# An S4 + MLP block on one core: packed parameters by way of DRAM in whole tiles, stores of u on two queues, and every DMA of the planned stage placed by the plan

## The chip, the core and the metric

The kernel runs on one NeuronCore of a Trainium2 chip. The metric is the device time of one execution in microseconds (us). Five engines work from instruction streams of their own, each in order: TensorE (PE, with its weight loads as PEld), VectorE (DVE), ScalarE (ACT), GpSimd (POOL) and SyncE (SP). SP and POOL here issue transfers for the most part; those are carried out by 16 DMA engines.

## The reference

One adaLN block over x of 2048 positions by 512 channels: a state-space convolution (S4) and an MLP with Mish, each behind a layer norm that is scaled, shifted and gated by a condition.

```python
mod = (silu(c) @ w_mod).reshape(1, 6, 1, -1)
sa, ca, ga, sb, cb, gb = (mod[:, i] for i in range(6))
h = layernorm(x) * (1 + ca) + sa
x = x + ga * A(h)
h = layernorm(x) * (1 + cb) + sb
return x + gb * (mish(h @ w1 + b1) @ w2)

def A(u):                                   # 512 channels d, 128 states n
    dt = exp(log_dt)
    P = exp(dt * (A_re + 1j*A_im) * arange(L))      # per d and n
    K = einsum("dn,dnl,dn->dl", C, P, dt * B).real  # the filter
    return causal_convolution(u, K) + u * Dskip     # by FFT over 2L
```

## The kernel before, in words

The 512 channels are four **blocks** of 128. For each block the kernel makes the filter's transform from the parameters, transforms u, multiplies the two, and transforms back; the results are added to x in DRAM (`x2d`). Then the MLP runs over four tiles of 512 positions. A first part of some 50 us (parameters of block 0, row statistics, the first modulation vectors) is written out by hand, and so is a `drain` (line 1154) that carries the last eight steps and leads over to the MLP. Between them lies the **planned stage**, which the change touches.

Its work is cut into operations of a few instructions, named by a short key and a number. Filter steps k = 0..31, eight to a block:

- `ang` k (TensorE, tile `pang`): angles of the powers, from the parameter tiles `S12` (in the trace all tiles `s...` go by the name `s`). `sin` k (ScalarE, into `ec`): three activations.
- `mag`, `comb` k (VectorE): `m` from `cf`, then four multiplications into `ec`. `cf` and `co` come from `vt` (TensorE, `pco`, from the tiles `S3`) and `va` (ScalarE, exponentials), four of each for a block.
- `kgen`, `ks`, `ka`, `tm` k (TensorE, ScalarE, TensorE, ScalarE): sums over states and the transform, kept in `gk`.

Convolution steps v = 0..31, eight to a block too, v being possible when filter steps 8b to 8b+7 of its block b are done:

- `gl` v (SP): load of `gu` from `ud`. `ubu`, `ug` v (TensorE `pub`, ScalarE): transform of u. `ubk` v (TensorE `pkb`): the last stage of the filter's transform.
- `prod` v (VectorE): two products and a sum, from `pkb` and `ug`. `t1`, `yt`, `invb`, `z` v: back-transform, and a store of `z` to `zd` in DRAM; `invb` uses the constants `mi` (`lm`, a load on POOL).
- per half block: `zl` (loads of `zt` from `zd`), `xp` (loads of x), `inva` (TensorE `pia`), `add` (VectorE) and the store to `x2d`.

Once, ahead of all `gl`: `ua` (TensorE `pua`) and `us` (ScalarE) make the first stage of u's transform in 32 pieces; each piece goes to `ud` in DRAM with two stores of 64 partitions, both on SP (line 773).

Parameters of blocks 1 to 3: `lp` loads the raw rows, `p0` to `p5` and `pa` (VectorE, with `p1` and the arctangent `pa` on ScalarE) compute them and write 12 rows for each of 128 partitions into the tile `pk`; `modp` rows (`mo`) are modulation vectors. `ls` spreads `pk` over the tiles `S3` and `S12`, whose partition is another one. For block 0 TensorE does that with selection matrices. For blocks 1 to 3 `ls` is 48 small copies from SBUF to SBUF on POOL: 32 for the first half of a block (lines 518 and 520, needed by its first `ang` and by `vt`) and 16 for the second.

**What sets the order.** `_plan` (line 57) is a list scheduler that runs on the host: each operation has an engine, a cost in `NS`, a place in `LEAD` or `AT` (smaller goes first), what it waits for with a lag, and the banks of PSUM that it takes. It hands back one sequence. The operations are then written out in that sequence, and for VectorE, ScalarE and TensorE a wrapper `InOrder` (line 286) holds the instructions to it. Transfers on SP and POOL were not held: they were issued inside the operation that makes their data (`z`, `us`, `add`), or stood in the plan at a cost near nothing (`gl`, `zl`, `lo`), and got their place in their queue from the framework's scheduler, by priority and its own estimates.

Of the kernel before, what the change touches and what calls it, by code (L numbers as in the profile page):

```python
# [39 lines left out]
NS = {"ang": 1400, "sin": 2900, "mag": 1140, "comb": 3570, "kgen": 1110, "ks": 270, "ka": 620, "tm": 560, "ubu": 1010,  # L40
      "ug": 770, "ubk": 1020, "prod": 1760, "t1": 590, "yt": 490, "invb": 1000, "z": 500, "inva": 1060, "add": 1210,
# [4 lines left out]
LEAD = {"ang": -1.72, "sin": -14.83, "mag": 4.37, "comb": 8.2, "kgen": 8.11, "ks": 1.94, "ka": -7.81, "tm":  # L46
        -0.64, "ubu": 15.3, "ug": 8.99, "ubk": 12.65, "prod": 4.12, "t1": 11.98, "yt": 10.08, "invb": 8.19, "z":
        11.51, "inva": 23.63, "add": 15.62}
AT = {"ua": -0.95, "un": 3.34, "nr": -2.74, "lf": 9.56, "na": 6.67, "sr": 0.11, "sg": 10.72, "st": -1.67,
# [3 lines left out]
SWITCH, HOP, LOAD, PART, TURN, STORE = 1280, 160, 4500, 2600, 5500, 3300  # L53
# [3 lines left out]
def _plan(k0):  # L57
    ops = {}

    def op(key, engine, pri, deps=(), banks=0, frees=None, table=None):  # L60
        ops[key] = (engine, NS[key[0]], pri, [d if len(d) == 3 else (*d, HOP) for d in deps], banks, frees, table)

# [36 lines left out]
    for v in range(nk - 6):  # L99
        op(("gl", v), "S", v + 5.6, [("ubu", v - 4) if v > 3 else ("mm", 0), ("us", 31, STORE)])  # L100
# [6 lines left out]
    for v in range(nk - 9):  # L107
# [11 lines left out]
    for b in range(1, nb):
        k = 8 * b  # L120
        if b:
# [160 lines left out]
def s4_block(ctx, tc, io, out):  # L282
    nc = tc.nc
    ordered = {key: None for key in "VAT"}
# [213 lines left out]

    def load_s(b, half):
        pk = PKR[b]  # L500
        for g in (half, 2 + half):
# [12 lines left out]
            for k in range(4):  # L514
                q = slice(32 * k, 32 * k + 32)
                if half == 0:
                    for i in (g, g + 1):
                        nc.gpsimd.dma_start(S3[b, i][q, :], pk[32 * i:32 * i + 32, 8 + k, :])  # L518
                for e in range(2):
                    nc.gpsimd.dma_start(S12[b, g][64 * e + 16 * k:64 * e + 16 * k + 16].rearrange("p h n -> p (h n)"),  # L520
                                        pk[d, k + 4 * e, :])
# [244 lines left out]
    def us(p):  # L766
# [5 lines left out]
        for h in range(2):  # L772
            US["last"] = nc.sync.dma_start(view(ud, (16 * a + 8 * h + g) * P, [[64 * P, 64], [64 * 64 * P, NB], [1, P]]),
                                           t[64 * h:64 * h + 64])

    def s_gl(v):
        b, s = divmod(v, 8)
        GU[v] = cv.tile([P, 512], F32, tag="gu", name=f"gu{v}", bufs=4).rearrange("p (r d) -> p r d", r=4)
        nc.sync.dma_start(GU[v], view(ud, (64 * b + 8 * s) * 64 * P, [[P, P], [P * P, 4], [1, P]]))
# [59 lines left out]
    def s_invb(v, whole=True):  # L839
# [703 lines left out]
```

## Time and profile before

| | us |
|---|---|
| median of 3 runs | 707.25 (706.45 to 708.76) |
| the profiled execution, its own time | 707.84 |
| its span, first to last instruction | 706.1 |
| first part, to the first row of the planned stage on VectorE | 0 to 49.7 |
| planned stage, to the last `add` | 49.7 to 343.9 |
| drain, to the first matmul of the MLP | 343.9 to 396.3 |
| MLP | 396.3 to 706.1 |

What the profiled execution takes beyond its span is 1.74 us. In the views, a row reads: start, length, engine, line, operation, output <- inputs with shapes, how many instructions; in brackets the idle time of that engine ahead of the row and what ended it. Nearly all rows have line 294, the wrapper's. A table of stretches gives, for each stretch, its length and the busy time of each engine with the number of instructions, then the granted clock of TensorE as a share, the share of the DMA engines and the rate. ScalarE and VectorE overlap the end of an instruction with the start of the next by some 0.1 us, so that lengths add up to a little more than the distance of starts.

### The profile page before, as it was taken

The page shows a single profiled execution, that of the slowest core. Times are in us where ns is not written, and L with a number is a line of the kernel's source. Part 1 is how long each engine was busy: PE and PEld are TensorE (multiplying, and loading weights), DVE is VectorE, ACT ScalarE, POOL GpSimd, SP SyncE. Part 2 cuts the span into 40 slices and gives each one's busy share as a digit, 9 for nine tenths or more (in the row PEclk, how much of TensorE's full clock was granted, in tenths as well). Part 3 has the DMA queues.
Part 4 walks back from the last instruction along what each step waited for, and adds up shares of the span by engine and source line. Part 5 has one row for each costly group of instructions (what it writes and reads, how often), then busy time and mean ns, then how long its engine had stood idle before and what let it go on. Part 6 is the DMA issues. An engine that isn't in the chain of part 4 may idle for free.

```text
span 706.1 us, 16609 instructions
## 1 busy us (share of the span) xinstructions
PE 616.7 (87%) x6722; PEld 497.4 (70%) x6722; DVE 478.5 (68%) x938; ACT 402.7 (57%) x705; POOL 102.0 (14%) x214
## 2 busy tenths in 40 slices
PE   0579796488888879899888999999999999999997
PEld 0445443367676657767786588889898888989996
DVE  7979961499869976979574899858237733563333
ACT  3677855488688856878572575453336234443231
POOL 2000058003900291000100000001001010010000
PEclk9968996699999997999999999999999999999999
DMA  9960579724435574764598799747433763264332
GB/s 251 219 256 15 138 200 213 234 78 127 113 107 139 146 178 128 195 173 121 157 277 260 230 320 298 244 142 225 129 102 93 205 176 94 90 180 144 96 90 59
DMA packets 108588, 117.31 MB, mean 166 GB/s; under 512 B 13408, under 2 KB 85472, under 8 KB 107360
## 3 DMA queue, kind: packets, MB, share of 16 engines
q1 hardware_dynamic: 93664, 85.61, 41.7%
q0 software_dynamic: 14464, 30.11, 15.2%
q8 instruction: 53, 0.87, 0.6%
q10 hardware_dynamic: 384, 0.52, 0.3%
q14 instruction: 23, 0.19, 0.1%
HBM read 81.36 MB, written 32.51 MB: 161 GB/s over the span
## 4 chain that ended last, share of the span: by engine, by line
PE 55%; DMA 13%; DVE 10%; issue 9%; ACT 7%; POOL 4%; SPq 1%; DVEq 0%; ACTq 0%; POOLq 0%
PE pr L294 31%; PE pp L294 11%; DVE ec L294 4%; DMA s<-pk 4%; ACT ec L294 3%; PE pang L294 3%; DMA zt<-zd 3%; DMA xr<-in_A_u 2%; POOL s L518 2%; PE pkg L294 2%; POOL s L520 2%; DVE q L294 2%; DMA zd<-z 2%; PE pib L294 1%; PE pia L294 1%
## 5 line engine op out<-in xcount | busy, mean ns | idle before, releaser
L294 PE MATMUL pr<-hh,w 128*128 128x256 f32 (+1 forms) x420 | 78.2, 327 | 0.5 <-ACT hh L294 0.5
L294 ACT ACTIVATE ec<-pang 128x1024 f32<-128x1024 f32 x64 | 62.3, 1027 | 27.0 <-PE pang L294 27.0
L294 PEld LDWEIGHTS pr<-hh,w 128*128 128x128 f32 x420 | 66.5, 188 | 12.7 <-ACT hh L294 1.9
L294 DVE TENSOR_TENSOR mh<-x,pr 128x256 f32<-128x256 f32 x63 | 26.4, 418 | 65.2 <-PE pr L294 64.9
L294 PE MATMUL pp<-w,mah 128*128 128x512 f32 x224 | 70.4, 396 | 0.0
L294 PE MATMUL pr<-w,mah 128*128 128x512 f32 x224 | 69.9, 393 | 0.0
L1265 POOL DMA_DIRECT2D w<-w2d x42 | 22.2, 528 | 301.7 <-PE pp L294 301.7
L294 DVE TENSOR_TENSOR ec<-ec,m 128x1024 f32<-128x1024 f32 x64 | 61.2, 957 | 3.5 <-ACT ec L294 1.0
L294 ACT ACTIVATE mh<-mh,b 128x256 f32<-128x256 f32 x63 | 32.1, 510 | 51.9 <-DVE mh L294 51.6
L294 ACT ACTIVATE mh<-pr,b 128x256 f32<-128x256 f32 (+1 forms) x35 | 19.4, 558 | 66.2 <-PE pr L294 66.2
L518 POOL DMA_DIRECT2D s<-pk x48 | 24.0, 503 | 181.4 <-PE pua L294 86.1
L294 DVE TENSOR_TENSOR m<-cf 128x1024 f32<-128x1024 f32 x32 | 38.9, 1217 | 16.4 <-ACT cf L294 16.4
L294 DVE TENSOR_TENSOR mal<-mh,mah 128x512 fp32r<-128x512 f32 x56 | 38.5, 688 | 14.6 <-ACT mah L294 14.5
L520 POOL DMA_DIRECT2D s<-pk x96 | 47.5, 501 | 4.9 <-DMA s<-pk 2.8
L294 PEld LDWEIGHTS pkg<-ec 128*32 128x32 f32 x2048 | 35.8, 117 | 16.5 <-issue 7.9
L294 PE MATMUL pkg<-ec 128*32 128x64 f32 x2048 | 41.0, 235 | 6.7 <-DVE ec L294 5.6
L294 PE MATMUL pub<-mf,gu 128*128 128x128 f32 x256 | 37.8, 294 | 10.4 <-issue 9.8
L294 ACT ACTIVATE ug<-pub,gd 128x512 f32<-128x512 f32 x64 | 34.0, 588 | 19.7 <-PE pub L294 19.5
L294 PE MATMUL pp<-w,mal 128*128 128x512 f32 x112 | 43.9, 392 | 0.0
L294 PE MATMUL pr<-w,mal 128*128 128x512 f32 x112 | 43.9, 392 | 0.0
L294 PEld LDWEIGHTS pub<-mf,gu 128*128 128x128 f32 x256 | 33.6, 204 | 13.0 <-issue 11.3
L294 PEld LDWEIGHTS pp<-w,mah 128*128 128x128 f32 x224 | 38.3, 189 | 4.9
(171 smaller groups left out, 1389.6 us busy)
## 6 DMA issues: line engine op xcount, KB each, us to landing
w<-w2d POOLq DMA_DIRECT2D x42, 512.0 KB, 3.6
ud<-us SPq DMA_DIRECT2D x64, 128.0 KB, 2.8
gu<-ud SPq DMA_DIRECT2D x32, 256.0 KB, 3.1
zd<-z SPq DMA_DIRECT2D x32, 256.0 KB, 2.7
zt<-zd SPq DMA_DIRECT2D x32, 256.0 KB, 5.2
w2d<-w SPq DMA_DIRECT2D x14, 512.0 KB, 4.1
xf<-x2d SPq DMA_DIRECT2D x16, 256.0 KB, 4.9
x2d<-xp SPq DMA_DIRECT2D x14, 256.0 KB, 3.6
```

The costliest lines, as they stand in the source:

```text
L294: ins = f(*a, **kw)
L518: nc.gpsimd.dma_start(S3[b, i][q, :], pk[32 * i:32 * i + 32, 8 + k, :])
L520: nc.gpsimd.dma_start(S12[b, g][64 * e + 16 * k:64 * e + 16 * k + 16].rearrange("p h n -> p (h n)"), pk[d, k + 4 * e, :])
L1265: nc.gpsimd.dma_start(t, w2d[f])
```

## The change

1. **`ls` by way of DRAM.** When `p5` has filled `pk`, a new operation `ps` stores the whole tile (128 partitions of 6 KB) to a DRAM buffer `pkd`, on SP. `ls` then loads whole tiles of 128 partitions from it on POOL: for the first half of a block four tiles `S3` and two tiles `S12`, for the second half two tiles `S12`. That is one store and eight loads for a block where there were 48 copies.
2. **Stores of u on two queues.** Of the two stores of a piece one is `ud` on SP, the other `up` on POOL.
3. **Every DMA is an operation.** `ud`, `up`, `zs` (store of z), `xs` (store to `x2d`) and `ps` are operations of their own, with costs; SP and POOL get an `InOrder` of their own, so that the plan's sequence is the queue's.
4. **Other numbers.** `NS`, `LEAD`, `AT` and the lags are new throughout, so that the sequence on every engine of the planned stage is another one. The arithmetic and the number of operations on VectorE, ScalarE and TensorE stay; ScalarE loads a table 12 times in both.

```diff
-LEAD = {"ang": -1.72, "sin": -14.83, "mag": 4.37, "comb": 8.2, ...
+LEAD = {"ang": 0.48, "sin": -8.01, "mag": 11.89, "comb": 2.1, ...
-SWITCH, HOP, LOAD, PART, TURN, STORE = 1280, 160, 4500, 2600, 5500, 3300
+SWITCH, HOP, LOAD, PART, TURN, STORE = 1280, 160, 4800, 3300, 5800, 3500
...
-            op(("us", p), "A", at + AT["us"], [("ua", g), ("us", p - 1), ("us", p - 8, STORE)], frees=[("ua", g)])
+            op(("us", p), "A", at + AT["us"], [("ua", g), ("us", p - 1), ("ud", p - 8, STORE), ("up", p - 8, STORE)],
+               frees=[("ua", g)])
+            op(("ud", p), "S", at + AT["us"], [("us", p)])
+            op(("up", p), "P", at + AT["us"], [("us", p)])
...
-        op(("gl", v), "S", v + 5.6, [("ubu", v - 4) if v > 3 else ("mm", 0), ("us", 31, STORE)])
+        op(("gl", v), "S", v + 5.6, [("ubu", v - 4) if v > 3 else ("mm", 0), ("ud", 31, STORE), ("up", 31, STORE)])
...
-        op(("z", v), "A", lead("z", v), [("invb", v)], frees=[("invb", v)])
+        op(("z", v), "A", lead("z", v), [("invb", v), ("zs", v - 3, STORE)], frees=[("invb", v)])
+        op(("zs", v), "S", v + 16, [("z", v)])
...
+            op(("xs", y + 5), "S", lead("add", y + 5), [("add", y + 5)])
...
-            op(("ls", 2 * b), "P", k + AT["ls"], [("p5", b), ("ang", k - 5), ("va", 4 * b - 1)])
+            op(("ps", b), "S", k + AT["p5"], [("p5", b)])
+            op(("ls", 2 * b), "P", k + AT["ls"], [("ps", b, LOAD), ("ang", k - 5), ("va", 4 * b - 1)])
...
-    ordered = {key: None for key in "VAT"}
+    ordered = {key: None for key in "VATSP"}
...
+    pkd = [dram.tile([P, 12, P], F32, name=f"pkd{b}") for b in range(NB)]
+
+    def store_p(b):
+        queue["S"].dma_start(pkd[b], PKR[b].bitcast(F32))
...
-            for k in range(4):
-                q = slice(32 * k, 32 * k + 32)
-                if half == 0:
-                    for i in (g, g + 1):
-                        nc.gpsimd.dma_start(S3[b, i][q, :], pk[32 * i:32 * i + 32, 8 + k, :])
-                for e in range(2):
-                    nc.gpsimd.dma_start(S12[b, g][64 * e + 16 * k:64 * e + 16 * k + 16].rearrange("p h n -> p (h n)"),
-                                        pk[d, k + 4 * e, :])
+            if half == 0:
+                for i in (g, g + 1):
+                    queue["P"].dma_start(S3[b, i], view(pkd[b], (32 * i * 12 + 8) * P, [[P, 4], [12 * P, 32], [1, P]]))
+            queue["P"].dma_start(S12[b, g], view(pkd[b], 32 * g * 12 * P, [[P, 8], [24 * P, 16], [12 * P, 2], [1, P]]))
...
+    def us_store(p, h):
+        g, a = UO[p // 4], p % 4
+        US["last", h] = queue["SP"[h]].dma_start(
+            view(ud, (16 * a + 8 * h + g) * P, [[64 * P, 64], [64 * 64 * P, NB], [1, P]]), US["t", p][64 * h:64 * h + 64])
...
+    queue.update(S=InOrder(nc.sync, "S"), P=InOrder(nc.gpsimd, "P"))
+    bulk[0] = queue["S"]
     for i, (_, (nm, n)) in enumerate(_plan(KO)):
```

After the planned stage `queue` points to the bare SP and POOL again; drain and MLP are written as before.

The places where the order shows the change, on engines that wait or are waited for. First POOL before: the end of the 48 copies of block 1 (`s3_1_...` and `s12_1_...` are its tiles `S3` and `S12`, `pk1` the packed tile) and what follows them.

```order
L518 DMA s3_1_2_1275<-pk1_430 32x128
L518 DMA s3_1_3_1276<-pk1_430 32x128
L520 DMA s12_1_2_1277<-pk1_430 16x2x128 x2
L520 DMA s12_1_1_1480<-pk1_430 16x2x128 x8
L520 DMA s12_1_3_1489<-pk1_430 16x2x128 x8
L989 DMA mi_1585<-in_mi 128x2048 x2
```

Both halves of the block stood together here, with the load of the constants behind them. The same place after, from the first transfer of block 1 on:

```order
L300 DMA s3_1_0_701<-pkd1_127 128x1x128
L300 DMA s3_1_1_702<-pkd1_127 128x1x128
L300 DMA s12_1_0_703<-pkd1_127 128x2x128
L300 DMA s3_1_2_707<-pkd1_127 128x1x128
L300 DMA s3_1_3_708<-pkd1_127 128x1x128
L300 DMA s12_1_2_709<-pkd1_127 128x2x128
L300 DMA ud_150<-us40_699 64x4x128
```

The first half is six transfers and stands ahead of the first store of u; the second half has moved away from it. VectorE before, around the first `prod` (`q<-pkb,ug0`), with `ec8` and `m28` of filter step 8 and `raw2` of block 2's parameters:

```order
L294 TENSOR_TENSOR m28_1600<-cf1_00_1573 128x1024
...
L294 TENSOR_TENSOR ec8_1531<-ec8_1531,co1_00_1572 128x32x32
L294 TENSOR_TENSOR m29_1633<-cf1_00_1573 128x1024
...
L294 TENSOR_SCALAR raw2_1254<-raw2_1254,ldt_79 128x128
L294 TENSOR_TENSOR q_1695<-pkb_1685,ug0_1630 128x512
```

The first product stood behind filter step 8 and a part of block 2's parameters. VectorE after, at the same `prod`:

```order
L300 TENSOR_TENSOR ec14_1953<-ec14_1953,co1_11_1360 128x32x32
L300 TENSOR_TENSOR q_2124<-pkb_2062,ug0_2039 128x512
L300 SCALAR_TENSOR_TENSOR q_2124<-pkb_2062,skip_89,ug0_2039 128x512
L300 TENSOR_TENSOR ug0_2039<-q_2124 128x2x4x64
L300 TENSOR_TENSOR m215_2163<-cf1_11_1361 128x1024
```

It now stands behind filter step 14; 17 filter steps are left beside the 24 products of the planned stage, where there were 23. SP after, the end of its 32 stores of u (`us33` is the last piece), with block 2's packed tile (`pk2`) among them, and the first loads of u (`gu`):

```order
L300 DMA pkd2_128<-pk2_1415 128x1536
L300 DMA wm1_1612<-in_w_mod 128x4x512
L300 DMA ud_150<-us23_1614 64x4x128
L300 DMA ud_150<-us30_1654 64x4x128
L300 DMA ud_150<-us31_1676 64x4x128
L300 DMA ud_150<-us32_1678 64x4x128
L300 DMA ud_150<-us33_1778 64x4x128
L300 DMA gu0_1868<-ud_150 128x4x128
```

The store of the packed tile is new there; it waits for VectorE and stands ahead of the last five of SP's stores of u.

More of the change, by code (lines that the diff above doesn't have):

```diff
@@ L39 @@
 ]
-NS = {"ang": 1400, "sin": 2900, "mag": 1140, "comb": 3570, "kgen": 1110, "ks": 270, "ka": 620, "tm": 560, "ubu": 1010,
-      "ug": 770, "ubk": 1020, "prod": 1760, "t1": 590, "yt": 490, "invb": 1000, "z": 500, "inva": 1060, "add": 1210,
+NS = {"ang": 1400, "sin": 2900, "mag": 1200, "comb": 3600, "kgen": 1110, "ks": 270, "ka": 620, "tm": 560, "ubu": 1050,
+      "ug": 940, "ubk": 1020, "prod": 1940, "t1": 590, "yt": 490, "invb": 1000, "z": 500, "inva": 1060, "add": 1210,
       "vt": 650, "va": 1420, "p1": 400, "p0": 2300, "p2": 1750, "p3": 1750, "pa": 200, "p4": 1250, "p5": 2100,
[3 rows of a table removed]
[L46 to L49, printed above, removed]
[3 rows of a table removed]
-SWITCH, HOP, LOAD, PART, TURN, STORE = 1280, 160, 4500, 2600, 5500, 3300
[3 rows of a table added]
+LEAD = {"ang": 0.48, "sin": -8.01, "mag": 11.89, "comb": 2.1, "kgen": 4.05, "ks": -3.04, "ka": 1.53, "tm":
+        -2.32, "ubu": 3.73, "ug": 8.79, "ubk": 9.62, "prod": 2.88, "t1": 11.73, "yt": 23.57, "invb": 11.53, "z":
+        16.66, "inva": 8.73, "add": 12.21}
+AT = {"ua": 0.79, "un": 1.7, "nr": 7.4, "lf": 6.84, "na": 10.19, "sr": -6.41, "sg": 9.94, "st": -7.3, "us":
[3 rows of a table added]
+SWITCH, HOP, LOAD, PART, TURN, STORE = 1280, 160, 4800, 3300, 5800, 3500
 UO, NA = (4, 5, 6, 7, 0, 1, 2, 3), (1,)
@@ L60, in op @@
     def op(key, engine, pri, deps=(), banks=0, frees=None, table=None):
-        ops[key] = (engine, NS[key[0]], pri, [d if len(d) == 3 else (*d, HOP) for d in deps], banks, frees, table)
+        ops[key] = (engine, NS.get(key) or NS[key[0]], pri, [d if len(d) == 3 else (*d, HOP) for d in deps], banks, frees, table)
     nk, nb = 8 * NB, NB
@@ L139, in _plan @@
     op(("sra", 0), "A", AT["sr"], [("srt", 0)], frees=[("srt", 0)])
-    op(("lm", 0), "P", 8, [("ang", 7), ("us", 31)])
+    op(("lm", 0), "P", 8, [("ang", 7), ("ud", 31), ("up", 31)])
     for i, n in ((i, AT[f"m{i}"]) for i in (1, 2, 4)):
@@ L361, in load_params @@
         raw[b] = t
-        nc.sync.dma_start(t[:, 0:6, :], io["par"][b].rearrange("p (k n) -> p k n", k=6))
+        queue["S"].dma_start(t[:, 0:6, :], io["par"][b].rearrange("p (k n) -> p k n", k=6))
+    queue = {"S": nc.sync, "P": nc.gpsimd}
     load_params(0)
@@ L771, in us @@
         A.copy(t.rearrange("p b d -> p (b d)"), US[g][a])
-        for h in range(2):
-            US["last"] = nc.sync.dma_start(view(ud, (16 * a + 8 * h + g) * P, [[64 * P, 64], [64 * 64 * P, NB], [1, P]]),
-                                           t[64 * h:64 * h + 64])
+        US["t", p] = t
+    def us_store(p, h):
+        g, a = UO[p // 4], p % 4
+        US["last", h] = queue["SP"[h]].dma_start(
+            view(ud, (16 * a + 8 * h + g) * P, [[64 * P, 64], [64 * 64 * P, NB], [1, P]]), US["t", p][64 * h:64 * h + 64])
     def s_gl(v):
@@ L845, in s_invb, with s_z @@
         if whole:
-            s_z(v)
-    def s_z(v):
+            s_z(v, True)
+    ZS = {}
+    def s_z(v, whole=False):
         b, s = divmod(v, 8)
@@ L851, in s_z, with z_store @@
         A.copy(z, PZ[v].rearrange("p (r d) -> p r d", r=4))
-        nc.sync.dma_start(view(zd[b], 8 * s * 64 * P, [[P, P], [P * P, 4], [1, P]]), z)
+        ZS[v] = z
+        if whole:
+            z_store(v)
+    def z_store(v):
+        b, s = divmod(v, 8)
+        queue["S"].dma_start(view(zd[b], 8 * s * 64 * P, [[P, P], [P * P, 4], [1, P]]), ZS[v])
     def zt_load(b, j4, a, r0, r1):
@@ L903, in inva_mm, with inva_add, x2_store @@
                          start=True, stop=True)
-    def inva_add(b, j):
+    def inva_add(b, j, whole=True):
         x = XP[b, j]
         V.tensor_add(x, x, PIA[b, j].rearrange("p (j d) -> p j d", j=4))
-        after(bulk[0].dma_start(x2d[b][:, 4 * j:4 * j + 4, :], x), pin.get("SP"))
+        if whole:
+            x2_store(b, j)
+    def x2_store(b, j):
+        after(bulk[0].dma_start(x2d[b][:, 4 * j:4 * j + 4, :], XP[b, j]), pin.get("SP"))
     XR = [None] * 16
@@ L1149, in s4_block @@
     tc.cur_priority = 100000 + 10000 * NG + 10000
-    for key in "VAT":
+    for key in "VATSP":
         ordered[key] = None
+    queue.update(S=nc.sync, P=nc.gpsimd)
     v0, vl = NG - 8, NG - 1
```

22 lines of the change are left out of this document (12 added, 10 removed), and 12 rows, old and new, of tables (AT, NS).

## The prediction

> **What bounds the kernel now.** I read the table of stretches first, cut where VectorE's rows show long waits, then the timelines of VectorE, TensorE, SP and POOL at those places. Columns of the stretches: length, then busy time of PE, PEld, DVE, ACT and POOL (with counts), granted clock, DMA share, GB/s.
>
> ```profile
> span 706.1 us, 16609 instructions
> ```
> ```profile
> 60.00:107.30 47.30, 40.33 (x845) 22.85 (x848) 40.05 (x71) 31.26 (x60) 11.09 (x23) 0.89 0.53 135
> 107.30:122.90 15.60, 9.41 (x44) 5.19 (x34) 0.01 (x1) 9.38 (x14) 13.75 (x28) 0.66 0.94 221
> 122.90:140.40 17.50, 7.72 (x90) 6.49 (x89) 8.20 (x15) 7.46 (x15) 0.00 (x0) 0.62 0.75 235
> 140.40:189.20 48.80, 41.24 (x768) 32.57 (x767) 47.50 (x70) 38.52 (x65) 17.85 (x36) 1.00 0.39 103
> 189.20:200.80 11.60, 10.70 (x166) 8.94 (x168) 4.95 (x7) 9.42 (x14) 5.88 (x12) 0.85 0.49 134
> 200.80:260.75 59.95, 49.46 (x978) 39.07 (x970) 58.11 (x89) 47.35 (x85) 17.03 (x35) 1.00 0.54 145
> 260.75:281.00 20.25, 18.77 (x194) 14.63 (x194) 9.31 (x14) 11.57 (x17) 6.69 (x14) 0.75 0.51 136
> 281.00:309.10 28.10, 25.41 (x441) 18.74 (x445) 24.04 (x28) 22.37 (x41) 0.00 (x0) 1.00 0.69 194
> 309.10:343.90 34.80, 33.33 (x702) 27.78 (x701) 32.25 (x40) 26.69 (x48) 0.00 (x0) 1.00 0.41 116
> 343.90:396.30 52.40, 45.17 (x469) 35.81 (x460) 31.85 (x72) 25.07 (x46) 3.33 (x6) 1.00 0.84 241
> 396.30:706.10 309.80, 304.42 (x1770) 266.17 (x1770) 173.03 (x385) 135.54 (x247) 22.19 (x42) 1.00 0.52 163
> ...
> 49.70:343.90 294.20, 246.06 (x4406) 182.59 (x4410) 234.33 (x354) 214.33 (x371) 72.29 (x146) 0.91 0.53 144
> ```
>
> The MLP (from 396.3) is TensorE's, 304.4 of 309.8 us, and nothing in the diff reaches it. In the planned stage VectorE is the engine to watch: 97% full in 140.4-189.2 and 200.8-260.75, but 234.33 us of work in 294.2. Of the 59.87 us idle, 42.48 lie in four rows of the table: 24.89 in 107.3-140.4 (33.1 less 8.21), 6.65 in 189.2-200.8, 10.94 in 260.75-281. These are the changes from one block's parameters to the next. VectorE's rows there:
>
> ```profile
> 43.97 1.22 DVE L294 TENSOR_TENSOR ec<-ec,co 128x1024 f32<-128x1024 f32 x1
> 49.71 0.16 DVE L294 TENSOR_SCALAR modp<-pmodp 128x4 f32<-128x4 f32 x1 [4.53 <-PE pmodp L294]
> ...
> 92.54 0.62 DVE L294 SCALAR_TENSOR_TENSOR raw<-raw 128x128 f32<-128x128 f32 x2 [3.67 <-ACT raw L294]
> ...
> 104.67 2.08 DVE L294 TENSOR_TENSOR raw<-raw 128x256 f32<-128x256 f32 x6 [2.32 <-DMA raw<-in_par]
> ...
> 122.89 1.22 DVE L294 TENSOR_TENSOR m<-cf 128x1024 f32<-128x1024 f32 x1 [15.62 <-ACT cf L294]
> ...
> 138.87 0.29 DVE L294 TENSOR_TENSOR raw<-raw 128x128 f32<-128x128 f32 x1 [8.97 <-ACT raw L294]
> ...
> 266.96 0.16 DVE L294 TENSOR_SCALAR modp<-pmodp 128x4 f32<-128x4 f32 x1 [6.21 <-PE pmodp L294]
> ...
> 275.87 1.28 DVE L294 TENSOR_TENSOR xp<-xp,pia 128x512 f32<-128x512 f32 x2 [3.16 <-PE pia L294]
> ```
>
> Behind them stand transfers. TensorE, then SP, then two groups of the page and one row of POOL:
>
> ```profile
> 114.29 0.97 PE L294 MATMUL pang<-ah,s 64*128 64x256 f32 x2 [6.18 <-DMA s<-pk]
> ...
> 135.17 2.04 PE L294 MATMUL pub<-mf,gu 128*128 128x128 f32 x8 [9.78 <-issue]
> ```
> ```profile
> 101.66 21.93 SPq L773 DMA_DIRECT2D ud<-us  x30
> 123.65 2.75 SPq L390 DMA_DIRECT2D xp<-in_A_u  x3
> 132.35 2.04 SPq L779 DMA_DIRECT2D gu<-ud  x4
> ```
> ```profile
> L518 POOL DMA_DIRECT2D s<-pk x48 | 24.0, 503 | 181.4 <-PE pua L294 86.1
> L520 POOL DMA_DIRECT2D s<-pk x96 | 47.5, 501 | 4.9 <-DMA s<-pk 2.8
> ```
> ```profile
> 111.77 8.82 POOL L520 DMA_DIRECT2D s<-pk  x18
> ```
>
> A copy costs POOL 0.5 us, so 32 for a half block take 16. TensorE's first `ang` of block 1 waits for them until 114.29, and in-order engines pass the wait on. Then a second wait comes, for u: SP issues its last 30 stores at 0.73 us each until 123.6, the first `gu` goes out at 132.35, `pub` starts at 135.17, and VectorE, with nothing else in its queue, stands until 140.4.
>
> **The change part by part.** The sum is for the profiled execution, 707.84 us, 0.59 above the median of 707.25. VectorE's work is the same in both orders, so I count its waits.
>
> *Parameters by DRAM.* The nearest rows for a store of 768 KB and for loads of 64 and 128 KB:
>
> ```profile
> zd<-z SPq DMA_DIRECT2D x32, 256.0 KB, 2.7
> w2d<-w SPq DMA_DIRECT2D x14, 512.0 KB, 4.1
> gu<-ud SPq DMA_DIRECT2D x32, 256.0 KB, 3.1
> ```
>
> From 256 to 512 KB a store takes 1.4 us longer, so 768 KB take 5.5; a load at most 3.1; six issues on POOL at 0.5 make 3.0: 11.6 us from `p5` to the first half block, where the 48 copies alone held POOL for 24. How long a filter step is on VectorE, from its `m` to the next product:
>
> ```profile
> 324.95 1.22 DVE L294 TENSOR_TENSOR m<-cf 128x1024 f32<-128x1024 f32 x1
> ...
> 329.88 0.68 DVE L294 TENSOR_TENSOR q<-pkb,ug 128x512 f32<-128x512 f32 x1
> ```
>
> That is 4.9 us. Block 1: `p3` to `p5` now stand right behind filter step 0, seven steps ahead of step 8. Block 2: `p5` stands behind step 9, six ahead of step 16; block 3 behind step 16, seven ahead of 24. Six steps are a cover of 29 us, so the round trip costs 0; without cover it would be 11.6 a block. What goes: in 107.3-140.4 the first wait, in 189.2-200.8 all 6.65, in 260.75-281 the 6.21 and its followers. In the last I leave out the 3.16 for `pia`, which hangs on the loads of `zt`, and 0.94 of small waits: 6.84.
>
> *Work in place of the wait for u.* The first `prod` has moved from behind filter step 8 to behind step 14. While u is stored, VectorE has the filter steps of block 1; with their `S` tiles early, those are free to run. So the second wait of 107.3-140.4 goes too: 24.89 in all. What is late next: u's stores must end before step 14 does. The last piece `us` stands on ScalarE ahead of `sin` 12, some three steps earlier (15 us), against 3.3 us from `gl` to `pub` for the load itself (132.35 to 135.17, 2.8). Two queues help: 32 stores on SP at 0.73 are 23 us where 64 were 47, and 32 on POOL at 0.5 are 16, beside nothing else there but `ls`. [...]
>
> ```profile
> ud<-us SPq DMA_DIRECT2D x64, 128.0 KB, 2.8
> ```
>
> SP's pace of 128 KB in 0.73 us is 180 GB/s, and the DMA engines, at a share of 0.94, moved 221 in 107.3-122.9. At 221 the 64 stores (8.4 MB) take 38 us, so two queues may bring 47 us down to 38 and not to 23. Either ends ahead of step 14, and the sum stands; that it does not is rival 3. [...]
>
> *Early parameters.* `p3`, `p4` (4.2 us by their instructions) now fill the 4.53 in front of 49.71; then `mo` and `p5` wait for `pmodp` and the arctangent on ScalarE. `pmodp`'s second set ended at 52.2:
>
> ```profile
> 51.15 1.05 PE L294 MATMUL pmodp<-mean,q 128*128 128x1 f32 x8 [0.37 <-ACT q L294]
> ```
>
> From 45.2 + 4.2 = 49.4 to 52.2 are 2.8 us of new wait. The 3.67 (arctangent, line at 92.54) and 2.32 (raw parameters, at 104.67) go: 6.0.
>
> *More products than steps.* 24 products share 17 filter steps; seven have none. In the drain products stand without filter steps:
>
> ```profile
> 362.09 0.69 DVE L294 TENSOR_TENSOR q<-pkb,ug 128x512 f32<-128x512 f32 x1 [0.43 <-PE pkb L294]
> ...
> 373.33 0.69 DVE L294 TENSOR_TENSOR q<-pkb,ug 128x512 f32<-128x512 f32 x1 [2.23 <-PE pkb L294]
> ```
>
> Between 0.43 and 2.23 each, 3 to 16 for seven; I take 1.0 each, 7, near the low end, because the plan has block 3's `p` operations between them.
>
> *TensorE's clock.* No row shows filter steps without products. In 60-107.3, with steps and u, TensorE was busy 40.33 of 47.3 at a granted clock of 0.89. At 0.64, as in 107.3-140.4, that work would take 56.1, 8.8 more than the stretch. So 0 to 8.8; I take 2, since u's matmuls thin out there. [...]
>
> *SP and POOL in order.* The same transfers, named; 0 where nothing is blocked (a rival below). Two loads of x2d for the MLP now stand at the end of the plan: 0.5 MB at 241 GB/s in the drain, whose DMA share is 0.84: 0 to 2.2, I take 2.
>
> Sum: 24.9 + 6.65 + 6.84 + 4.5 + 6.0 = 48.9 gained; 2.8 + 7 + 2 + 2 = 13.8 lost; 35.1 net. 707.84 - 35.1 = 672.7, on the median 672. With the waits of 3.16 and 0.94 gone too and the low ends: 660; with all high ends (2.8 + 15.6 + 8.8 + 2.2): 688.
>
> **The rivals.**
> 1. *Other engines are as full.* In the compressed stage ScalarE has 214.33 us and TensorE 246.06 (at low clocks in part) beside VectorE's 234.33. If VectorE is filled only as in 281-309.1 (24.04 of 28.1, 85.6%), 234.33 takes 273.7, from 45.2 to 318.9: 25 gained against 343.9, less 2 in the drain, 684. For it: that stretch holds products, `va` and `zt` together, as the new order does throughout. Against: 97% in the two stretches of 109 us.
> 2. *Fuller than thought.* At 97%, 241.6 us, to 286.8: 57 gained, 650. Against: the `pia` waits.
> 3. *u late.* `ud` behind the store of `pk2`, which waits for VectorE, and `up` behind block 2's `ls`: if `gl` comes so late that step 14 ends first, the 24.9 are spent again: 697.
> 4. *z's queue, slower than before.* A store of z now stands behind a load of `gu` that waits for a free buffer, and `z` three steps on waits for that store. The one such wait before:
>
> ```profile
> 377.53 0.58 ACT L294 COPY z<-pib 128x512 f32<-128x512 f32 x1 [3.18 <-DMA zd<-z]
> ```
>
> At 3.18 each, 11 of 23 stores eat the gain; all would make 746. It decides when a store is held for longer than some three steps (with a product each 4.9 + 2.1 us, so 21) less its 2.7. Nothing in the trace comes near that, but no queue was bound so before.
> 5. *Nothing changes*, the wait for parameters being replaced whole by one on `zt` or ScalarE: 707.
>
> **How the numbers follow.** A measurement of this kernel can tell about 0.3%, 2.1 us. Forecast (660 to 688) 0.58; rival 1 (684) 0.19; rival 2 (650) 0.06; rival 3 (697) 0.05; rival 4 0.08; rival 5 0.04. Faster 0.88, same 0.04, slower 0.08. From 657 to 697 the range leaves out rivals 2, 4 and 5, 0.18.
>
> **What would show it.** Right: VectorE near-continuous from filter step 1 to 16; no wait for `s` on TensorE at blocks 1 to 3; the first `gu` issued before step 14 ends; the last `comb` near 305 to 310; drain and MLP within 2 us of 52.4 and 309.8. Wrong: ScalarE's `z` or `us` ended by a DMA many times (rival 4); `pub` waiting at the first product (3); TensorE at 0.6 in block 1 (clock); the MLP's length changed at all.

## The result and the profile after

| | before | after |
|---|---|---|
| median of 4 runs (lowest to highest) | 708.0 (706.45 to 709.42) | 685.32 (680.64 to 686.88) |
| the profiled execution, its span | 707.84, 706.1 | 685.72, 683.9 |
| planned stage, to the last `add` or `comb` | 343.9 | 322.9 |
| drain | 52.4 | 50.7 |
| MLP | 309.8 | 310.3 |

After over before is 0.967, with a 95% interval of 0.962 to 0.972: 23 us faster, where 35 were forecast. Of the 22.2 us by which the span is shorter, 21.0 lie in the planned stage, 1.7 in the drain, and the MLP gives 0.5 back. So the sum has to be compared in the planned stage. The stretch from the end of the row at 43.97 (45.19) to the end of the stage, before:

```profile
45.19:343.90 298.71, 249.94 (x4430) 184.04 (x4426) 234.33 (x354) 218.84 (x376) 72.29 (x146) 0.91 0.53 144
```

And after:

```profile
45.19:322.90 277.71, 244.34 (x4408) 177.86 (x4400) 234.51 (x355) 217.57 (x377) 40.71 (x58) 0.91 0.62 166
```

VectorE's work is the same, 234.3 and 234.5. Its idle time fell from 64.4 to 43.2 us; the forecast's sum would have left 64.4 - 37.1 = 27.3 (48.9 gained, less 2.8, 7 and 2 in this stretch). The 16 us between 43.2 and 27.3 are what has to be found. The view of waits groups them by what ended them. Columns: tile, what it waited for, us in total, how often, the longest. VectorE before, in this stretch:

```profile
DVE m L294 <- ACT cf L294: 16.4, 3, 15.6
DVE raw L294 <- ACT raw L294: 12.6, 2, 9.0
DVE modp L294 <- PE pmodp L294: 12.3, 3, 6.2
DVE q L294 <- PE pkb L294: 9.5, 3, 4.9
DVE xp L294 <- PE pia L294: 3.2, 1, 3.2
DVE raw L294 <- DMA raw<-in_par: 2.3, 1, 2.3
DVE ec L294 <- ACT ec L294: 1.0, 2, 0.6
```

VectorE after:

```profile
DVE q L300 <- PE pkb L300: 17.1, 5, 5.9
DVE ec L300 <- ACT ec L300: 9.9, 4, 4.6
DVE m L300 <- ACT cf L300: 6.2, 1, 6.2
DVE modp L300 <- PE pmodp L300: 2.1, 1, 2.1
```

The waits for ScalarE's rows of parameters (`raw`, 12.6), for the raw parameters' load and for `pia` are gone; those for `cf` and `modp` are 10 us shorter each. Against that the products wait 7.6 us more for `pkb` and the filter steps 8.9 more for the sine (`ec`). Where these stand, in VectorE's timeline after:

```profile
86.29 1.95 DVE L300 TENSOR_TENSOR ec<-ec,m 128x1024 f32<-128x1024 f32 x2 [1.21 <-ACT ec L300]
...
96.17 1.95 DVE L300 TENSOR_TENSOR ec<-ec,m 128x1024 f32<-128x1024 f32 x2 [4.60 <-ACT ec L300]
...
109.06 1.23 DVE L300 TENSOR_TENSOR m<-cf 128x1024 f32<-128x1024 f32 x1 [6.23 <-ACT cf L300]
...
145.94 1.95 DVE L300 TENSOR_TENSOR ec<-ec,m 128x1024 f32<-128x1024 f32 x2 [3.60 <-ACT ec L300]
...
165.52 0.69 DVE L300 TENSOR_TENSOR q<-pkb,ug 128x512 f32<-128x512 f32 x1 [5.85 <-PE pkb L300]
...
178.46 0.69 DVE L300 TENSOR_TENSOR q<-pkb,ug 128x512 f32<-128x512 f32 x1 [3.95 <-PE pkb L300]
...
271.43 0.69 DVE L300 TENSOR_TENSOR q<-pkb,ug 128x512 f32<-128x512 f32 x1 [5.89 <-PE pkb L300]
```

Three things are to be seen. Between 85 and 109 VectorE waits 12.0 us for ScalarE (1.21, 4.60, 6.23), at filter steps 6 to 8. At 165.52 the first product waits 5.85 us: u is late. At 178.46 and 271.43 products stand at a block change with no filter step between them, and wait for `pkb`. No wait of VectorE is ended by a DMA, and none of TensorE is ended by a parameter tile.

The place between 85 and 109, first ScalarE, then TensorE (the many small products of the transform of the filter left out):

```profile
86.15 0.37 ACT L300 COPY gk<-pkg 128x256 f32<-128x256 f32 x1
...
91.33 0.37 ACT L300 COPY ks<-pkg 128x256 f32<-128x256 f32 x1 [3.56 <-PE pkg L300]
91.60 1.08 ACT L300 COPY us<-pua 128x512 f32<-128x512 f32 x2
93.17 1.94 ACT L300 ACTIVATE ec<-pang 128x1024 f32<-128x1024 f32 x2 [0.49 <-PE pang L300]
```
```profile
83.81 1.07 PE L300 MATMUL pua<-xr,bdu 32*64 32x512 f32 x2
86.57 1.90 PE L300 MATMUL pua<-xr,bdu 32*64 32x512 f32 x8 [1.70 <-ACT gk L300]
...
89.68 1.57 PE L300 MATMUL pkg<-ec 128*32 128x64 f32 x64
```

This is a ring of waits over two in-order engines. The first-stage transform of u (`ua`) needs four banks of PSUM (its four tiles `pua`) and gets its second one when ScalarE has copied the last filter step's sums out (`gk`, done at 86.52). The sums of the next step (`kgen`, at 89.68) stand behind `ua` on TensorE. ScalarE waits 3.56 us for them, then copies two pieces of u, then makes the next sine, and only behind the sine comes the next `gk`. One turn, from 86.57 to the same place of the next step at 96.46, is 9.9 us, where VectorE needs 4.9 for the step.

The late u, first POOL, then SP:

```profile
135.23 0.73 POOL L300 DMA_DIRECT2D s<-pkd  x1
140.13 1.64 POOL L300 DMA_DIRECT2D s<-pkd  x2 [4.17 <-issue]
142.32 0.69 POOL L300 DMA_DIRECT2D s<-pkd  x1 [0.55 <-issue]
143.92 1.68 POOL L300 DMA_DIRECT2D s<-pkd  x2 [0.91 <-issue]
145.59 0.69 POOL L300 DMA_DIRECT2D ud<-us  x1
```
```profile
149.99 14.92 SPq L300 DMA_DIRECT2D gu<-ud  x6
```

The last store of u on POOL went out at 145.59, behind the six loads of block 2's first half, though ScalarE had its piece ready at 141.4 (a copy of 0.59 us from 140.82). The first `gu` could be loaded at 149.99 only, when VectorE was 9.7 us from the end of filter step 14 (159.67). From there it took 7.8 us to `pub` (157.81) and 15.5 to the first product.

### The profile page after: what moved, and what is told of

Same layout as the page of the kernel before. It is cut to its first block, busy times and chain, and to the rows that moved or that the text cites. A ratio compares the mean times of both kernels' runs of the same rounds, so it can differ in the third digit from the quotient of the medians.

```text
span 683.9 us, 16472 instructions
## 1 busy us (share of the span) xinstructions
PE 613.0 (90%) x6722; PEld 492.8 (72%) x6722; DVE 478.6 (70%) x938; ACT 401.1 (59%) x705; POOL 70.5 (10%) x126
## 4 chain that ended last, share of the span: by engine, by line
PE 61%; DVE 19%; issue 8%; ACT 5%; DMA 4%; POOL 2%; SPq 0%; DVEq 0%; POOLq 0%; ACTq 0%
PE pr L300 31%; PE pp L300 11%; DVE ec L300 6%; PE pang L300 4%; PE pkg L300 3%; DVE q L300 3%; DVE raw L300 3%; PE pub L300 2%; ACT ec L300 2%; PE pkb L300 2%; PE pib L300 2%; DVE m L300 2%; PE pia L300 2%; PE pt L300 1%; DMA gu<-ud 1%
## 5 line engine op out<-in xcount | busy, mean ns | idle before, releaser
L300 PEld LDWEIGHTS pr<-hh,w 128*128 128x128 f32 x420 | 66.6, 188 | 12.6 <-ACT hh L300 1.9
L300 DVE TENSOR_TENSOR ec<-ec,m 128x1024 f32<-128x1024 f32 x64 | 61.3, 958 | 12.6 <-ACT ec L300 9.9
L1293 POOL DMA_DIRECT2D w<-w2d x42 | 22.2, 530 | 298.5 <-PE pp L300 197.1
L300 PEld LDWEIGHTS pkg<-ec 128*32 128x32 f32 x2048 | 37.1, 120 | 21.3 <-issue 17.7
L300 PE MATMUL pkg<-ec 128*32 128x64 f32 x2048 | 42.4, 240 | 8.4 <-issue 4.3
L300 DVE TENSOR_TENSOR x<-x,pr 128x256 f32<-128x256 f32 x42 | 17.6, 419 | 34.3 <-PE pr L300 34.3
L300 DVE TENSOR_TENSOR q<-pkb,ug 128x512 f32<-128x512 f32 x32 | 22.0, 687 | 27.9 <-PE pkb L300 26.1
L300 PEld LDWEIGHTS pr<-hh,wt 128*128 128x128 f32 x252 | 35.6, 190 | 5.4 <-DVE mh L300 2.0
```

What stands on the lines that cost most here:

```text
L300: ins = f(*a, **kw)
L1293: nc.gpsimd.dma_start(t, w2d[f])
```

## The experiments

The theory after the result: the gain is the order of the work, and what is missing was lost in the ring of 85 to 109 and in u's last store. The rivals: the way by DRAM is the gain; the second queue is; the clock of TensorE is what was lost. Each run was timed beside runs of the kernel before, and is given as a ratio to it with its 95% interval. The changed kernel, run once more as a yardstick:

> The changed kernel once more, on the chip of the runs beside it, as their yardstick: 681 to 687 us.

685.5 us, ratio 0.972 (0.968 to 0.977).

**One queue for u.**

```diff
-        US["last", h] = queue["SP"[h]].dma_start(
+        US["last", h] = queue["S"].dma_start(
```

> The changed kernel with both stores of u on SP; VectorE's, ScalarE's and TensorE's sequences unchanged. Theory A (the pieces us are paced by ScalarE and TensorE at 2 us a piece and more, so a queue that takes 1.46 us for the two stores of a piece keeps up): 684 to 688 us, the first load of u within 2 us of 150 in the trace. Theory B (the second queue is what brings u early enough): u ends 5 to 10 us later, the first product waits that much longer, 690 to 695. Theory C (the two queues crowd the 16 DMA engines and hold up the 4.26 us of TensorE in 135.5-139.8): that stall goes, 681 to 683.

680.3 us (679.8 to 685.5), ratio 0.965 (0.961 to 0.969): not theory B, and faster than either A or the changed kernel itself. Theory C came nearest in time, and fails in the trace: TensorE's stall in the middle of a step's sums was still there, 4.34 us. What went was the wait at the first product, from 5.85 to 0.77: the first `gu` went out at 148.86, where the changed kernel had 149.99, though VectorE was 2.7 us later in this profile from 54.33 on. So the second queue, which was to bring u earlier, made it later.

**The copies back.** The eight loads become the 48 copies again, and `ps` does nothing.

```diff
-        queue["S"].dma_start(pkd[b], PKR[b].bitcast(F32))
+        pass
...
-            if half == 0:
-                for i in (g, g + 1):
-                    queue["P"].dma_start(S3[b, i], view(pkd[b], ...))
-            queue["P"].dma_start(S12[b, g], view(pkd[b], ...))
+            for k in range(4):
+                ...
+                queue["P"].dma_start(S3[b, i][q, :], pk[32 * i:32 * i + 32, 8 + k, :])
+                ...
+                queue["P"].dma_start(S12[b, g][64 * e + 16 * k:64 * e + 16 * k + 16]..., pk[d, k + 4 * e, :])
```

> The changed kernel with the 48 small copies a block on POOL in place of the store and the eight loads by DRAM; the sequences else unchanged. Theory A (most of the gain is the order, the parameters stand far enough ahead): 32 copies at 0.5 us hold POOL 16 us for a first half, so the first stores of u come some 8 us later and the last one some 6 us later than with the six loads; 690 to 698 us. Theory B (the way by DRAM is the gain): the waits of VectorE for the parameters come back at three block changes, 705 us or more.

692.9 us, ratio 0.981 (0.977 to 0.986), in theory A's range. POOL, and VectorE's first product, of this kernel:

```profile
140.52 14.05 POOL L300 DMA_DIRECT2D s<-pk  x28 [2.06 <-DMA ud<-us]
154.57 0.65 POOL L300 DMA_DIRECT2D ud<-us  x1
```
```profile
174.27 0.69 DVE L300 TENSOR_TENSOR q<-pkb,ug 128x512 f32<-128x512 f32 x1 [13.71 <-PE pkb L300]
```

With the one store of u behind the copies, the first product waits 13.71 us, 7.9 more than with the loads. No wait of TensorE ends with a parameter tile.

**The order alone.** Both edits above together, so that only the sequence is new.

> The changed kernel's order alone: the 48 copies a block on POOL and both stores of u on SP. Theory A (the order is the gain, POOL has only the copies and is free of u): 685 to 692 us, no wait of TensorE for a parameter tile over 3 us. Theory B (the order lives on the new ways): 700 us or more, with waits of TensorE for the parameter tiles at the block changes as before.

678.6 us (678.1 to 679.4), ratio 0.961 (0.958 to 0.965): faster than the changed kernel, whose nine runs (680.6 to 687.2) all lie above these four, though its first interval (0.962 to 0.972) just overlaps this one. No wait of TensorE ends with a parameter tile. Three of VectorE's waits in it:

```profile
109.47 1.23 DVE L300 TENSOR_TENSOR m<-cf 128x1024 f32<-128x1024 f32 x1 [6.23 <-ACT cf L300]
...
171.08 0.69 DVE L300 TENSOR_TENSOR q<-pkb,ug 128x512 f32<-128x512 f32 x1 [2.93 <-PE pkb L300]
...
264.10 0.69 DVE L300 TENSOR_TENSOR q<-pkb,ug 128x512 f32<-128x512 f32 x1 [5.89 <-PE pkb L300]
```

The wait at the first product is gone; the waits in 85 to 109 (1.22, 4.61, 6.23) and at the last block change are as in the changed kernel. The order is the whole gain; the other two parts together cost some 4 to 8 us, by the two ratios of the changed kernel.

**DRAM alone, in the old order.** The kernel before with the store and the eight loads.

```diff
+    pkd = [dram.tile([P, 12, P], F32, name=f"pkd{b}") for b in range(NB)]
...
-            for k in range(4):
-                ...
+            if b and (b, "d") not in S3:
+                S3[b, "d"] = nc.sync.dma_start(pkd[b], PKR[b].bitcast(F32))
+            if half == 0:
+                for i in (g, g + 1):
+                    nc.gpsimd.dma_start(S3[b, i], view(pkd[b], ...))
+            nc.gpsimd.dma_start(S12[b, g], view(pkd[b], ...))
```

> The kernel before with the parameters by DRAM alone (one store on SP, eight loads on POOL a block), its order and the stores of u unchanged. Theory A (the steps of the prediction): in block 1 the wait for parameters goes, but the wait for u behind it, which ends at 140.4 whatever the parameters do, takes nearly all of it; 6.65 go at block 2 and 6.84 at block 3: 13 us gained, 693 to 696. Theory B (nothing but the parameters stood in the way): 25 us or more gained, 682 or less. Theory C (other waits replace them): 705 to 708.

700.6 us, with wide runs (694.9 to 706.6), ratio 0.990 (0.984 to 0.995): between theories A and C, some 3 to 11 us. VectorE at block 1, in the profile of the shortest run (694.9):

```profile
123.53 1.23 DVE L294 TENSOR_TENSOR m<-cf 128x1024 f32<-128x1024 f32 x1 [15.29 <-ACT cf L294]
...
137.66 0.29 DVE L294 TENSOR_TENSOR raw<-raw 128x128 f32<-128x128 f32 x1 [7.12 <-ACT raw L294]
```

The first wait stays at 15.29 where it was 15.62. The store went out at 99.94 and the first half's last load at 111.9: where nothing covers it, the way by DRAM takes 12 us from store to last issue and gains nothing on the copies. My expectation that this wait would go and u's would take its place was wrong; both stayed.

Nor could a faster way have gained much here. In the old order ScalarE copies out all 32 pieces of u before the first sine of block 1, and the last nine of these copies waited 7.4 us in all for buffers that a store of u had to empty. ScalarE in the kernel before, the last copy and that sine:

```profile
114.52 0.58 ACT L294 COPY us<-pua 128x512 f32<-128x512 f32 x1 [0.68 <-DMA ud<-us]
117.00 1.94 ACT L294 ACTIVATE ec<-pang 128x1024 f32<-128x1024 f32 x2 [1.90 <-PE pang L294]
```

So until 115.1 it was copies of u, paced by their stores, that held ScalarE, and the exponentials for `cf` stand behind this sine; the parameters, late on TensorE until 114.29, held it for 1.9 us more (1.92 with DRAM alone). Of the 15.62, faster parameters alone could have saved about these 1.9, an estimate from the rows shown. The new order has 11 of the 32 copies behind this sine, and no copy of u in it waits for a store. In the rest of this trace, 3.35 of the 6.21 at block 3 and most of the 3.16 for `pia` (0.54 left) went, and the waits at block 2 stayed (1.06 and 4.89 where they were 1.60 and 4.94).

**One swap on POOL.** Block 2's loads wait for the last store of u; in the plan's sequence that exchanges two neighbours on POOL and nothing else.

```diff
-            op(("ls", 2 * b), "P", ..., [("ps", b, LOAD), ("ang", k - 5), ("va", 4 * b - 1)])
+            op(("ls", 2 * b), "P", ..., [("ps", b, LOAD), ("ang", k - 5), ("va", 4 * b - 1)] + ([("up", 31)] if b == 2 else []))
```

> The changed kernel with one swap on POOL: the last store of u ahead of the six loads of block 2's first half; all other sequences the same. Theory A (u is late because that store stands behind the loads, which wait for TensorE and for their turn): the store goes out at 141.4 instead of 145.6, the first load of u at 146 instead of 150, some 4 of the 5.85 us of VectorE's wait at the first product go; 680 to 682. Theory B (u is late because two queues crowd the 16 DMA engines): the first load of u stays at 150, 685. Theory C (block 2's tiles come later and its first angles wait): 685 or more, TensorE waiting for a parameter tile.

680.3 us, ratio 0.963 (0.958 to 0.968): theory A. POOL, then SP:

```profile
141.40 0.62 POOL L300 DMA_DIRECT2D ud<-us  x1 [5.48 <-ACT us L300]
```
```profile
144.50 14.34 SPq L300 DMA_DIRECT2D gu<-ud  x6
```

The store went out at 141.40 and the first `gu` at 144.50, 5.5 us earlier; the wait at the first product is gone. That the two queues with this swap (680.3) and one queue (680.3) take the same time says that the second queue is worth nothing by itself.

**The cost of `ua`.** In the plan it is 1.4 us; in the trace the part behind its wait alone takes 3.2 in the ring (86.57 to 89.76). With 3.2 the planner puts `kgen` ahead of `ua`. It also moves some operations on the other engines by a few places, among them block 2's loads on POOL, which now stand ahead of the last four stores of u and not of one.

```diff
-      "sc": 2600, "nr": 520, "ua": 1400, "us": 580, ...
+      "sc": 2600, "nr": 520, "ua": 3200, "us": 580, ...
```

> The changed kernel with the plan's cost of a first-stage transform of u at 3.2 us, as measured between 75 and 106, instead of 1.4: the sums of a filter step now stand ahead of it on TensorE. Theory A (the two in-order engines pass their waits to each other: the sums stand behind the transform of u, which waits for ScalarE to empty its banks): ScalarE's 3.56 us of wait in each step go, a step of 9.9 us takes 7 to 8, and of VectorE's 12 us of waits in 85-109 some 8 go; 675 to 679. Theory B (TensorE is full there at the clock it is granted, 8.3 of 10 us at 0.84): the wait only moves to the angles, 683 to 687.

673.8 us (671.5 to 675.0), ratio 0.955 (0.951 to 0.959): 11.7 us less than the changed kernel, theory A. ScalarE, then VectorE:

```profile
76.37 1.94 ACT L300 ACTIVATE ec<-pang 128x1024 f32<-128x1024 f32 x2 [0.24 <-PE pang L300]
...
82.74 1.94 ACT L300 ACTIVATE ec<-pang 128x1024 f32<-128x1024 f32 x2 [0.23 <-PE pang L300]
```
```profile
102.43 1.22 DVE L300 TENSOR_TENSOR m<-cf 128x1024 f32<-128x1024 f32 x1 [4.11 <-ACT cf L300]
```

A step takes 6.4 us instead of 9.9, no `ks` waits in the ring, and VectorE's three waits of 12.0 are down to 5.06: 0.95 for a sine at 92.12 and this one of 4.11. The wait of 3.60 at 145.94 is gone too. u ended earlier; the wait at the first product (3.49 us) did not go altogether, since the steps ended earlier as well.

**Both together.** The order alone with the cost of 3.2, and the same with the parameters by DRAM:

> The order alone (copies on POOL, both stores of u on SP) with the same cost of 3.2 us for the transform of u. By theory A the two changes add: 678.6 less 8, 669 to 673. By theory B: 677 to 680.

670.6 us (669.7 to 674.0), ratio 0.951 (0.947 to 0.955).

> Parameters by DRAM, both stores of u on SP, and the cost of 3.2 us for the transform of u: the same as the run of 670.6 us but for the way of the parameters. Theory A (with this order either way is hidden: 24 us of copies and 12 us by DRAM both lie under the 29 us of cover): 669 to 673 us. Theory B (the eight larger loads are worth something even so, since 40 fewer issues leave POOL and the DMA engines to others): under 668. Theory C (the store of the packed tile delays the stores of u behind it on SP): 674 or more.

670.7 us (669.0 to 673.7), ratio 0.952 (0.948 to 0.955). Theory A in both times, and the way of the parameters makes no difference. The gains do not add in full: 6.9 for the order alone and 11.7 for the cost would be 18.6, and 14.9 came. That fits the run with the cost alone, where only 3.49 us were left at the first product to be gained. These two are the fastest versions, 35 us under the kernel before and 15 under the changed one.

**Queues not held.** The order alone, with SP and POOL left to the framework's scheduler as before.

```diff
-    queue.update(S=InOrder(nc.sync, "S"), P=InOrder(nc.gpsimd, "P"))
-    bulk[0] = queue["S"]
```

> The order alone (copies on POOL, both stores of u on SP), and SP and POOL no longer held to the plan's sequence; VectorE's, ScalarE's and TensorE's sequences unchanged. Theory A (the order of the three engines is the gain): 677 to 683 us. Theory B (the queues in order are a good part of it): 688 or more, with loads of gu or stores of z that come late.

682.4 us (678.4 to 686.2), ratio 0.967 (0.963 to 0.971), beside 0.961 (0.958 to 0.965) with the queues held. Theory A; holding the queues may be worth a few us, which these intervals, just overlapping, don't settle.

**The clock.** In 74 to 106 the granted clock was 0.84 in the changed kernel and 0.95 with the cost of 3.2. To have the ring at the full clock, extra matmuls were put into `ua`, into a bank that is overwritten afterwards.

```diff
+                if (h, a) == (0, 1):
+                    for _ in range(4):
+                        T.matmul(ps[0][64:128, :], bdu, XR[8 + g], start=True, stop=False, skip_group_check=True)
```

> The changed kernel with four matmuls of 64 columns by 128 rows into a bank that is overwritten afterwards, in each transform of u, at the place where TensorE waits 1.7 us for banks (work that is not needed; the result is the same). Theory A (the waits let the granted clock fall to half, and TensorE at half clock makes the loop of 9.9 us): the granted clock in 74-106 goes from 0.84 to over 0.95, a step takes 8 to 8.5 us, 4 to 6 us gained: 679 to 682. Theory B (the loop is the order of the two engines, whatever the clock): a step stays at 9.9 us or grows by what the extra matmuls overrun, 685 to 690.

711.9 us, ratio 1.009 (1.006 to 1.013): neither theory; they stood at the wrong place. A float32 matmul counts as two in these rows (x128 for the 64 of `pua`), so the wait comes behind the first matmul and not behind the second, and the four ran after it. TensorE, in this run's profile (which at 720.2 us is 8 above its median):

```profile
91.29 1.07 PE L300 MATMUL pua<-xr,bdu 32*64 32x512 f32 x2
94.06 8.20 PE L300 MATMUL pua<-xr,bdu 32*64 32x512 f32 x16 [1.70 <-ACT gk L300]
```

They took 6.8 us of a turn that grew by 5.2. What it does show is that TensorE's time inside `ua` reaches the end: eight longer `ua` made the kernel 26 us longer. The second attempt puts two of them behind the first matmul (`(h, a) == (0, 0)`, `range(2)`).

> The changed kernel with two such extra matmuls in each transform of u, now right behind its first matmul, so that they run inside the 1.7 us in which TensorE waits for banks (work that is not needed; the result is the same). In the run before, the extra matmuls took 6.8 us of a step that grew by 5.2, so what is left of the step was 1.6 us shorter at the full clock. Theory A (clock): the granted clock in 74-106 is 0.95 or more and a step takes some 8.3 us instead of 9.9; VectorE's 12 us of waits in 85-109 fall by 4 to 5; 680 to 682. Theory B (the order of the two engines alone): 685 to 687, a step of 9.9. Theory C (the extra work overruns the wait): 688 or more.

687.1 us (685.1 to 692.1), ratio 0.975 (0.970 to 0.980). Theory A in the clock and the step, theory C in the time. VectorE, and the stretch 74 to 106 of this kernel:

```profile
93.61 1.95 DVE L300 TENSOR_TENSOR ec<-ec,m 128x1024 f32<-128x1024 f32 x2 [3.55 <-ACT ec L300]
...
101.98 1.95 DVE L300 TENSOR_TENSOR ec<-ec,m 128x1024 f32<-128x1024 f32 x2 [3.09 <-ACT ec L300]
```
```profile
74.00:106.00 32.00, 32.00 (x514) 15.33 (x512) 22.19 (x27) 21.91 (x37) 10.91 (x17) 1.00 0.55 143
```

The same stretch of the changed kernel, then of the one with the cost of 3.2:

```profile
74.00:106.00 32.00, 24.63 (x418) 12.82 (x410) 22.44 (x31) 20.53 (x35) 10.18 (x16) 0.84 0.54 139
```
```profile
74.00:106.00 32.00, 26.52 (x560) 16.75 (x552) 26.12 (x42) 28.45 (x51) 11.86 (x18) 0.95 0.59 157
```

At a clock of 1.00 a turn takes 8.37 us (93.61 to 101.98) instead of 9.9. TensorE is busy for all 32 us here, so the extra work could itself have set the 8.37. The run with one queue speaks against that: it has no extra work and the changed kernel's sequence, and one of its turns (90.64 to 99.01) is as long:

```profile
90.64 1.95 DVE L300 TENSOR_TENSOR ec<-ec,m 128x1024 f32<-128x1024 f32 x2 [2.81 <-ACT ec L300]
...
99.01 1.95 DVE L300 TENSOR_TENSOR ec<-ec,m 128x1024 f32<-128x1024 f32 x2 [3.09 <-ACT ec L300]
```

The granted clock of that turn is not shown here, so the split is an estimate from these turns: of the 3.5 us by which the changed kernel's turn is longer than the 6.4 of the better order, 1.5 are the clock and 2.0 the order itself. The better order has most of both: its granted clock there was 0.95, and TensorE was busy for 26.52 of the 32 us, where the changed kernel had 24.63. The total did not gain: the extra matmuls also lengthen `ua` in the steps ahead of 85, where the changed kernel had no wait, and the first product waited 7.64 us.

## Why the prediction came out as it did

The time lay in the range and the likeliest case named the right direction; the gain was two thirds of the forecast. That it fell below the forecast's upper end, 688, is in part luck: that end was the sum of high losses for products (15.6) and the clock (8.8), and what was lost was lost elsewhere. Luck too is rival 1's 684, the number nearest to the 685.3: VectorE was busy for 234.5 of 277.7 us, 84.4% where rival 1 took 85.6%, but it meant engines that are as full, and the same work took 670.6 in another order. Point by point, by its own steps:

- *The second wait of 107.3-140.4 goes too, 24.89 in all*: the step that was mis-sized. 12.8 went. At the same filter step VectorE still waited 6.23 for `cf` (109.06, 15.62 before), and at the first product 5.85 for u. The 6.23 is not the parameters': the exponentials stood behind a sine that came late. 2.1 of it went with the better order of the ring, and 4.11 stayed.
- *Behind them stand transfers* (parameters, then u): the first wait was read from TensorE's row alone. By ScalarE's rows it was copies of u until 115.1, and the parameters for 1.9 us of it. The wait went all the same, since the new order no longer has all copies of u ahead of block 1's sine; so 15.62 of the sum stood under the wrong heading.
- *u stored in time* (rival 3): "`up` behind block 2's `ls`" is what happened, and the swap on POOL shows it. That the 24.9 would then be spent again was too much: 5.85 were. The last `us` did stand three steps ahead of step 14, but its store did not. And the load was too cheap: the prediction has 3.3 us from `gl` to `pub` (2.8 by the rows beside it), where 7.8 were measured, and 15.5 from `gl` to the first product. So its sign, a first `gu` before step 14 ends, came true (149.99 against 159.67) and the product waited all the same.
- *ScalarE and TensorE keep up*, costed at nothing without saying so: 12.0 us in 85 to 109. The 6.0 counted for the arctangent and the raw parameters went as said, and the new waits for the sine took their place. The plan's table had the number to check against the trace: `ua` 1.4, measured 3.2. Rival 1 spoke of engines that are full; ScalarE was busy for 20.5 of 32 us there and TensorE for 24.6. It was their order, not their load, apart from the 1.5 us a turn that the estimate above gives to the clock.
- *TensorE's clock, 0 to 8.8, 2 taken*: by the estimate above 1.5 us a turn at 0.84, within the bounds. The granted clock fell to 0.50 behind pauses of 1.70 us (ended at 76.98, 86.57 and 96.46).
- *Seven products without filter steps, 7*: with the 4.6 for `pkb` of before that the sum left standing (2.80 and 1.76) the forecast came to 11.6; apart from u's, 17.1 - 5.85 = 11.3 were measured. Right in sum, and by luck: they fell on two block changes (3.95 and 0.41, 5.89 and 1.01) rather than on seven products.
- *6.65 at block 2 and 6.84 at block 3*: the rows for `pmodp` are gone, as were the 3.16 for `pia` and the 0.94 that I had left in. But 4.94 of the 6.65 was a wait for `pkb`, not for parameters; DRAM alone left it at 4.89, and in the new order 3.95 and 0.41 stand at that change, counted in the line above.
- *2.8 for `modp`*: 2.15. *Two loads of x2d, 2*: the drain became 1.7 shorter. *z's queue* (rival 4): no wait of `z` or `us` was ended by a DMA. *The last `comb` near 305 to 310*: it ended at 322.9.
- *One turn more*: 3.60 at 145.94 follows a stop of TensorE, below.
- *Parameters by DRAM cost 0*: right, and so did the copies. The prediction had the number for it: a cover of 29 us hides 24 us of copies as well as 12 by DRAM. It put 38 us of gains under "Parameters by DRAM" and "Work in place of the wait for u"; what came of them the order alone has, and in the old order DRAM alone left the wait at 15.29.
- *Two queues help*: they added nothing (680.3 with two and the swap, 680.3 with one), and cost 5 us through a neighbour on POOL.

In sum 16 us were missing from the idle time of VectorE: 12.0 in 85 to 109, 5.85 for u, 3.60 at 145.94 and 0.45 beside it, less the 4.1 at block 3 that it had left in (3.16 and 0.94) and the 2 for the clock, which is in the ring. That is 15.8.

## What to carry to other kernels

When a change brings both a cheaper transfer and a new order, first ask whether the order alone already hides the old transfer; here it hid both, and what the new ways did was to put one store behind six loads. A cost in a planner's table is worth one look at the trace: one number, 1.4 against 3.2 us, was worth 12 us, more than either of the new transfers. Before a wait is put down to a transfer, read the rows of every engine on the way to it: here the engine in between, ScalarE, was held by another transfer for as long. Where two in-order engines feed each other, count one turn of the ring, bank releases too, and not only how full each of them is.

## What the runs showed of the hardware

The granted clock of TensorE fell to 0.50 without a pause above 2.27 us. In the changed kernel that was its longest in 74 to 106, and the pauses of 1.70 came with one lone matmul (the row of 1.07 us) ahead of them; the granted clock went between 1.00 and 0.50 in the rhythm of the ring (0.50 in 77 to 80, 88 to 90 and 98 to 100). With the pause filled by the two extra matmuls it stayed at 1.00 in that stretch. A pause of this length did not always do it: in the changed kernel the clock was 1.00 in 126 to 138, past a pause of 1.70 that ended at 130.24 with three matmuls (a row of 1.08 us) ahead of it, and in the kernel before it was 1.00 in 216 to 226, past one of 2.01 that ended at 219.40. In the changed kernel, from 108 to 124, it stayed at 0.50 for 16 us in which TensorE's rows show it busy for 15.5.

TensorE also stopped in the middle of a step's sums (`kgen`, 64 equal rows of matmuls), with nothing in the profile that it waited for:

```profile
139.81 0.68 PE L300 MATMUL pkg<-ec 128*32 128x64 f32 x16 [4.26 <-issue]
```

POOL stood still at the same time (4.17, above), and the DMA engines were at a share of 1.0 to 1.1 in 134 to 138. One packet of a queue that the profile calls "instruction" fell into 134 to 141. The stop was 2.31 to 4.34 us in the runs with the changed kernel's sequence on TensorE, and at most 1.70 in those with `kgen` ahead of `ua`. What caused it was not shown.
